# First MLP layer by seven block products, tiles of 512 tokens, decoding in steps: a spectral mixer and MLP on one core

## The chip, the cores and the metric

The kernel runs on one core of a Trainium2 chip. The metric is the time of one execution on the device, in microseconds (us). PE is the engine of matmuls (PEld its weight loads), DVE the vector engine, ACT the scalar (activation) engine, POOL the GpSimd engine, SP the engine that issues the DMAs. SBUF is the memory that the engines work in, PSUM the small one that matmuls write to, in eight banks of 512 float32 columns.

## The reference

There are 8 batches of 3136 tokens with 256 channels. First a spectral stage, then an MLP with a low-rank mixing of tokens (`x` is the output of the first for the second):

```
X = np.fft.rfft(x, axis=1)
Yr = Xr @ w_r - Xi @ w_i + b_r
Yi = Xr @ w_i + Xi @ w_r + b_i
Yr = np.sign(Yr) * np.maximum(np.abs(Yr) - 0.01, 0.0)      # Yi likewise
y  = np.fft.irfft(Yr + 1j * Yi, n=3136, axis=1)

h = xt @ U @ V                       # xt: x with tokens last; U (3136, 32), V (32, 3136)
u = x + h.transpose(0, 2, 1)
ch = np.maximum(u @ w_ch1, 0.0) @ w_ch2      # w_ch1 (256, 1024), w_ch2 (1024, 256)
return u + ch
```

U, V, w_ch1 and w_ch2 come as float64; the kernel turns their words into float32 itself ("decoding").

## The kernel before, in words

Every matmul that needs float32's accuracy is done as three in a cheaper format: an operand is split into a high part (a copy, on ACT) and a low part (the difference, on DVE or POOL), and `mm3` adds high x high, low x high and high x low (lines 93, 94, 95; in the trace these lines stand for all users of the helper, the tiles tell them apart). `split` (lines 82 and 85) makes the two parts.

A batch passes through these stages. **a**: the first step of the transform, 16 units of two of the 32 columns of tokens (`psa`, stored through `gs` to DRAM `gd`). **b**, **mix**, **c**: 12 or 13 pairs `q` of frequencies; `b_unit` loads `t` and the table `fb`, multiplies (`psb`), copies the result out (`xs`), adds real and imaginary parts (`ts`) and splits all three; `mix_unit` does the complex product with the weights by three products (`pst`, `psq`), adds the bias (`tb`), and the shrinking by ACT (`rl`) and DVE (`ys`); `c_unit` does a further step (`psc`) and stores to `zd`. **d**: 32 units (`psd`) finish the inverse transform into `xq` and add up `pa`, the product with U. **MLP**: a tile is 392 tokens (4 x 98); `v_unit` adds the product with V (`psv`) and splits u into `uh`, `ul`; `l1` does one eighth of the first layer, 6 matmuls of 392 columns into `psh`, then ACT takes the relu (`rh`) and DVE its low part (`rlo`, out of PSUM); `l2`, two steps later, does 6 matmuls into the two banks `pso` that gather all eight; at the end `ot` adds u, `os` is transposed, and the result goes out.

The main loop runs over 8 batches x 8 tiles x 8 steps. Beside each step's `l1` and `l2` it emits "side" units: the next batch's b, mix, c (pairs over steps 0 to 36 of 64), a of the batch after, and d (36 to 54). A scheduler then orders all instructions of each engine by a model of their times; on the chip each engine works its list in that order. `behind` and `issue_after` fix an order against it. So batch 0's spectral stage and the decoding have no MLP beside them: this is the run-up, up to the first `psh`.

In the run-up, `decode` takes the words of one piece (`dw`) through 2 operations on ACT and 6 on DVE, or one and one more where the piece is split at once (`dm`, `dlf`, `dq`, `dp`). The pieces of V go to DRAM (`vfl`) and come back spread (`v4`) for `make_v`, which fills `vs`, V for all tokens, in SBUF. U's pieces make `us`; `make_ud` (`psu`) multiplies it into the table of stage d. Four of the eight pieces of the MLP's weights are decoded before the first `psh`, four after it. PSUM has three banks `psf` for the spectral stages, three `psm` (`psh`, `psv`) and the two `pso`.

Of the kernel before, what the change touches and what calls it, by code (L numbers as in the profile page):

```python
# [21 lines left out]
NB = 8  # L22
N1, N2 = 49, 64
NP = 98
# [5 lines left out]
TOK = TI * NP  # L30
# [8 lines left out]
FILL_1, FILL_2, IDLE = 4, 4, 7  # L39
WHOLE_A = {(0, u) for u in range(1, 16)} | {(1, u) for u in range(16)}  # L40

@with_exitstack
def fft_mix_moe_kernel(
# [25 lines left out]
    ps_m = ctx.enter_context(tc.tile_pool(name="ps_m", bufs=3, space=PSUM))  # L69
    ps_o = ctx.enter_context(tc.tile_pool(name="ps_o", bufs=1, space=PSUM))  # L70
    fp = ctx.enter_context(tc.tile_pool(name="fp", bufs=2))
    qp = ctx.enter_context(tc.tile_pool(name="qp", bufs=2))

# [37 lines left out]
    w1s = [const.tile([128, 2, 1024], F32R, name=f"w1{k}") for k in "hl"]  # L111
# [7 lines left out]
    vs = const.tile([128, NI, NP], F32R, name="vs")  # L119

    xv = x.rearrange("b (p i) d -> b p i d", i=NI)

    ov = out.rearrange("b n (a d) -> b a n d", a=4)
    ob = ov[:, :, 0 : 96 * NI].rearrange("b a (p g t) d -> b a t p g d", g=12, t=NT)
    ol = ov[:, :, 96 * NI :].rearrange("b a (q i) d -> b a i q d", i=NI)
    rest = {}
# [4 lines left out]
    first_w = {}  # L131

    def a_load(b, u, ahead=False):
        if ahead:
            xt = qp.tile([NP, 2, D], F32, tag="xq", name=f"xt_{b}_{u}", bufs=10)
        else:
            xt = fp.tile([NP, 2, D], F32, tag="xt", name=f"xt_{b}_{u}")

        late = b == 1 and u >= FILL_1
        with tc.issue_after(s_state[0, "zl"].ins) if late else nullcontext():  # L140
            dma.dma_start(xt, xv[b, :, 2 * u : 2 * u + 2, :])
        a_state[b, u, "x"] = xt

    def a_prep(b, u):
# [6 lines left out]
        xh = fp.tile([NP, 2, D], F32R, tag="xh", name=f"xh_{b}_{u}")  # L151
        xl = fp.tile([NP, 2, D], F32R, tag="xl", name=f"xl_{b}_{u}")
# [3 lines left out]
    def a_mm(b, u):  # L156
# [5 lines left out]
        tg = "xs" if b == 0 and u % 2 else "gs"  # L162
# [10 lines left out]
    def a_units(b):  # L173
        us = []
        for u in range(NI // 2 + 1):
            def unit(u=u):
                if u < NI // 2:
                    a_prep(b, u)
                if u > 0:
                    a_mm(b, u - 1)  # L180
            us.append(unit)
# [17 lines left out]
    def load_fb(b, q):  # L199
# [3 lines left out]
        tg = "fb" if b else ("fb", "th", "tl")[q % 3]  # L203
        fbt = fp.tile([128, 2, 128], F32, tag=tg, name=f"fb_{b}_{q}", bufs=2)
# [19 lines left out]
    def ybuf(b, q, tag):  # L224

        tg, bufs = (tag, 1) if b else (dict(rl="xsh", ys="xsl")[tag], 2)
        return fp.tile([128, 2, D], F32, tag=tg, name=f"{tag}_{b}_{q}", bufs=bufs)

    def b_mm(b, q):
# [3 lines left out]
        pl, tg = (ps_f, "psf") if b else (ps_m, "psm")  # L233
        ps = pl.tile([128, 2, 2, 128], F32, tag=tg, name=f"psb_{b}_{q}")
# [14 lines left out]
    def b_unit0(q):  # L249
        n = pairs(0)[q][1]  # L250
        ps = b_mm(0, q)
        xx = []
        for k in "hl":
            xx.append(qp.tile([128, 2, 2, 3, 64], F32R, tag="xq", name=f"x3{k}_{q}", bufs=10))
        xh, xl = xx
# [13 lines left out]
    def mix_unit0(q):  # L269
        n = pairs(0)[q][1]  # L270
        xx = s_state.pop((0, q, "x"))
        pl, tg = ((ps_f, "psf"), (ps_m, "psm"))[q % 2]
        ps = pl.tile([128, 2, D], F32, tag=tg, name=f"psy_{q}")
# [16 lines left out]
        yh = fp.tile([128, 2, D], F32R, tag="yh", name=f"yh_0_{q}")  # L290
        yl = fp.tile([128, 2, D], F32R, tag="yl", name=f"yl_0_{q}")
# [4 lines left out]
    def b_unit(b, q):  # L296
# [6 lines left out]
        xs = fp.tile([128, 2, 2, 2, 64], F32, tag="xs", name=f"xs_{b}_{q}")  # L303
        for h in range(2):
            acopy(xs[:, h, :, 0:n, :], psv[:, h, :, 0:n, :])
        ts = fp.tile([128, 2, 2, 64], F32, tag="ts", name=f"ts_{b}_{q}", bufs=1)
        pool.tensor_tensor(
            out=ts[:, :, 0:n], in0=xs[:, :, 0, 0:n], in1=xs[:, :, 1, 0:n], op=ALU.add
        )
        xh = fp.tile([128, 2, 2, 2, 64], F32R, tag="xsh", name=f"xsh_{b}_{q}")  # L310
        xl = fp.tile([128, 2, 2, 2, 64], F32R, tag="xsl", name=f"xsl_{b}_{q}")
# [723 lines left out]
```

## Time and profile before

| | |
|---|---|
| median of 3 runs | 1788.68 us (1786.59 to 1791.38) |
| profiled execution | 1784.9 us, span from first to last instruction 1783.1 |
| granted clock of PE | 0.99 |
| PE busy | 1754.8 us, 98% |
| DVE, ACT, POOL busy | 1004.1, 876.7, 546.0 us (56, 49, 31%) |
| DMA | 192 MB, 38% of the 16 engines' time |
| first `psh` | 145 us after the start |

A row of a group reads: line, engine, operation, out<-in, shapes, count | busy us, mean ns of one | idle time before them and what ended it. A row of the timeline reads: start in us, length, engine, line, operation and shape; x2 means that two were merged. In the chain of work that ended last a row has start, length, engine, tile and line.

### The profile page before, as it was taken

What the parts mean: (1) busy time and instruction counts of PE and PEld (TensorE: products, weight loads), DVE (VectorE), ACT (ScalarE), POOL (GpSimd) and SP (SyncE); (2) the same over time, 40 slices, a digit from 0 to 9 for tenths busy, and PEclk for the clock granted to TensorE, in tenths of its full rate; (3) what the DMA queues carried; (4) which work ended last, traced back from release to release, by engine and by line L of the source; (5) the groups of instructions that cost most, each with busy time, mean ns of one, the idle gap of its engine ahead of it and who ended that gap; (6) DMA issues with size and microseconds to landing.
All of it is one profiled execution on the core that took longest, in us unless ns stands there. A gap on an engine that the chain in (4) does not pass through costs nothing.

```text
span 1783.1 us, 30104 instructions
## 1 busy us (share of the span) xinstructions
PE 1754.8 (98%) x10755; PEld 1687.0 (95%) x10755; DVE 1004.1 (56%) x1942; ACT 876.7 (49%) x1879; POOL 546.0 (31%) x583
## 2 busy tenths in 40 slices
PE   8989999999999999999999999999999999999998
PEld 5877999999999999999999999999999999999997
DVE  2667666456643567447653377645664357644443
ACT  3756565455445565344545566444554555443232
POOL 1212453133314464113322455313331334211110
PEclk9979999999999999999999999999999999999999
DMA  7775443423245453322324445332224533240001
GB/s 239 209 224 179 141 135 98 112 77 84 56 120 148 144 156 103 106 69 75 80 74 140 143 139 152 87 101 66 78 63 111 149 102 94 51 118 22 23 23 28
DMA packets 285546, 192.46 MB, mean 108 GB/s; under 512 B 167874, under 2 KB 257222, under 8 KB 285202
## 3 DMA queue, kind: packets, MB, share of 16 engines
q1 hardware_dynamic: 285398, 190.54, 38.4%
q8 instruction: 86, 1.41, 0.3%
q14 instruction: 62, 0.51, 0.1%
HBM read 112.59 MB, written 77.87 MB: 107 GB/s over the span
## 4 chain that ended last, share of the span: by engine, by line
PE 89%; DMA 4%; DVE 3%; SPq 1%; ACT 1%; issue 1%; POOL 0%; DVEq 0%; ACTq 0%; POOLq 0%
PE pso L95 10%; PE psh L93 10%; PE pso L94 10%; PE psh L95 10%; PE pso L93 10%; PE psh L94 10%; PE psd L449 6%; PE psb L237 4%; PE psq L93 2%; PE psq L95 2%; PE psq L94 2%; DMA gd<-gs 1%; PE psv L820 1%; PE psa L94 1%; PE psa L93 1%; PE psa L95 1%
## 5 line engine op out<-in xcount | busy, mean ns | idle before, releaser
L838 DVE SCALAR_TENSOR_TENSOR rlo<-psh,rh 128x392 fp32r<-128x392 f32 x512 | 284.9, 561 | 329.0 <-ACT rh L837 326.4
L837 ACT ACTIVATE rh<-psh 128x392 fp32r<-128x392 f32 x512 | 252.3, 496 | 353.5 <-PE psh L95 271.6
L93 PE MATMUL psh<-uh,w1h 128*128 128x392 f32 x1024 | 352.8, 345 | 0.1
L95 PE MATMUL psh<-uh,w1l 128*128 128x392 f32 x1024 | 350.7, 343 | 0.0
L94 PE MATMUL psh<-ul,w1h 128*128 128x392 f32 x1024 | 350.5, 342 | 0.0
L94 PE MATMUL pso<-rlo,w2h 128*128 128x392 f32 x1024 | 350.2, 342 | 0.0
L95 PE MATMUL pso<-rh,w2l 128*128 128x392 f32 x1024 | 350.2, 343 | 0.0
L93 PE MATMUL pso<-rh,w2h 128*128 128x392 f32 x1024 | 334.0, 346 | 0.0
L85 POOL TENSOR_TENSOR yl<-ys,yh 128x512 fp32r<-128x512 f32 (+1 forms) x101 | 130.9, 1296 | 314.8 <-ACT yh L82 312.5
L85 POOL TENSOR_TENSOR ul<-xq,uh 128x392 fp32r<-128x392 f32 x126 | 133.3, 1067 | 282.2 <-ACT uh L82 282.0
L357 DVE SCALAR_TENSOR_TENSOR ys<-tb,rl 64x256 f32<-64x256 f32 x350 | 181.3, 518 | 61.0 <-ACT rl L353 57.2
L93 PEld LDWEIGHTS pso<-rh,w2h 128*128 128x128 f32 x1024 | 191.2, 188 | 5.8 <-issue 0.7
L93 PEld LDWEIGHTS psh<-uh,w1h 128*128 128x128 f32 x1024 | 192.4, 188 | 4.4 <-DVE rlo L838 0.5
L94 PEld LDWEIGHTS pso<-rlo,w2h 128*128 128x128 f32 x1024 | 192.6, 188 | 3.7
L95 PEld LDWEIGHTS pso<-rh,w2l 128*128 128x128 f32 x1024 | 192.4, 188 | 2.7 <-DVE rlo L838 0.3
L94 PEld LDWEIGHTS psh<-ul,w1h 128*128 128x128 f32 x1024 | 192.6, 188 | 2.4
L95 PEld LDWEIGHTS psh<-uh,w1l 128*128 128x128 f32 x1024 | 192.5, 188 | 2.0 <-issue 0.5
L85 POOL TENSOR_TENSOR xl<-xt,xh 98x512 fp32r<-98x512 f32 x96 | 129.3, 1347 | 169.8 <-ACT xh L82 162.1
L82 ACT ACTIVATE xq<-psd 128x196 f32<-128x196 f32 x256 | 85.1, 335 | 116.2 <-PE psd L449 102.8
L353 ACT ACTIVATE rl<-tb,lam 128x512 f32<-128x512 f32 x88 | 63.5, 721 | 123.3 <-DVE tb L350 123.1
L449 PE MATMUL psd<-dt,zt 98*128 98x130 f32 x896 | 121.2, 274 | 0.0
L449 PEld LDWEIGHTS psd<-dt,zt 98*128 98x128 f32 x896 | 118.9, 190 | 0.0
(161 smaller groups left out, 2920.2 us busy)
## 6 DMA issues: line engine op xcount, KB each, us to landing
xt<-in_x_dram SPq DMA_DIRECT2D x128, 196.0 KB
gd<-gs SPq DMA_DIRECT2D x128, 196.0 KB
zt<-zd SPq DMA_DIRECT2D x128, 196.0 KB
t<-gd SPq DMA_DIRECT2D x192, 128.0 KB
zd<-zs SPq DMA_DIRECT2D x192, 128.0 KB
out_dram<-os SPq DMA_DIRECT2D x256, 96.0 KB
fb<-in_fb_dram SPq DMA_DIRECT2D x96, 128.0 KB
dt<-in_fd_dram SPq DMA_DIRECT2D x56, 150.1 KB
```

The source lines that it names most:

```text
L82: return act.activation(o, i, AF.Copy)
L85: return eng.tensor_tensor(out=o, in0=a, in1=b, op=ALU.subtract)
L93: pe.matmul(o, lhsT=l[0], rhs=r[0], start=first, stop=False)
L94: pe.matmul(o, lhsT=l[0], rhs=r[1], start=False, stop=False)
L95: return pe.matmul(o, lhsT=l[1], rhs=r[0], start=False, stop=last)
L237: pe.matmul(ps[:, h, k, :], lhsT=t[:kk, k, h * 128 : h * 128 + 128], rhs=fbt[:kk, k if k0 else 0, :], start=True, stop=True,)
L353: act.activation(rl[:m], yv[:m], AF.Relu, bias=lam[:m])
L357: dve.scalar_tensor_tensor(out=ys[64 * c : 64 * c + 64, k, :], in0=yv[64 * k : 64 * k + 64, c, :], scalar=LAM, in1=rl[64 * k : 64 * k + 64 ...
L449: pe.matmul(psv[:, h, :], lhsT=zt[:, i % 2, 128 * h : 128 * h + 128], rhs=dt_[:, k, :], start=True, stop=True,)
L820: mm = pe.matmul(ps[:, 0:TOK], lhsT=pt[:, 128 * h : 128 * h + 128], rhs=vt, start=True, stop=True)
L837: act_ = act.activation(rh, o, AF.Relu)
L838: dve_ = dve.scalar_tensor_tensor(out=rl, in0=o, scalar=0.0, in1=f32(rh), op0=ALU.max, op1=ALU.subtract)
```

## The change

**First layer.** With the weight as 2 x 2 blocks (output features in halves of 512, input channels in halves of 128) and a window of 512 tokens as 2 x 2 (channels by token halves of 256), the first layer is done by Winograd's form of Strassen's method: seven block products of 512 features x 128 channels x 256 tokens, where before there were eight. Sums of weight blocks are made once (`combine`, into `w1t`, seven blocks, high and low). Sums of the token blocks are made for each window: t1 = b12 - b11, t2 = b22 - t1, t3 = b22 - b12, t4 = b21 - t2 (`tt`), and these and b11, b21, b22 are split into `oa`, `ob`, `oc`, `od`. A product is still three matmuls for each 128 features. The products are added up partly in PSUM (`psx`, `psy`, `psz`, a bank each) and partly by ACT's copies (`s5`, `s1`, `v12`) and DVE's additions; then the relu and its low part, whose input is now in SBUF for three of four. The features are done in two halves `g`; each half has four chunks c0 to c3, and between them stand the four chunks of the second layer of the half before.

**Windows.** 98 = 96 + 2 rows of tokens: six windows of 16 x 32 tokens for a batch; the remaining 2 x 32 tokens of all batches are gathered in DRAM (`rd`, by `rest_unit`, `psr`) and make a 49th window at the very end. u stays in `xq` (half a batch each, three buffers), and V is loaded for each window (`vw`) from DRAM `vd`, where it lies split.

**Spectral stages.** `b_unit` copies the high parts straight out of PSUM, and DVE makes the low parts and `ts` out of PSUM too (before, ACT copied `xs` and POOL added `ts`). Buffers `xh`, `xl`, `xsh`, `xsl`, `th`, `tl`, `yh`, `yl` are single. The a units of batch 1 are unsplit for 8 of 16, before for all. Side units have other places among 96 slots a batch.

**Decoding.** It is a generator that gives way after one to three instructions; the run-up takes three steps of it behind each pair's mix, eight more behind the last, and one behind every other d unit. All weights are decoded before the first layer starts; a load is issued three jobs ahead.

```
-TOK = TI * NP
+TOK = 512
+HT = TOK // 2
...
-FILL_1, FILL_2, IDLE = 4, 4, 7
-WHOLE_A = {(0, u) for u in range(1, 16)} | {(1, u) for u in range(16)}
+FILL_1, FILL_2, IDLE, STEPS_W = 4, 4, 7, 8
+WHOLE_A = {(0, u) for u in range(1, 16)} | {(1, u) for u in range(FILL_1 + FILL_2)}
...
+        for h in range(2):
+            acopy(xh[:, h, :, 0:n], vs[h])
+            acopy(ts[:, h, 0:n], vs[h][:, 0])
+        for h in range(2):
+            sub(dve, xl[:, h, :, 0:n], vs[h], f32(xh[:, h, :, 0:n]))
+            dve.tensor_tensor(out=ts[:, h, 0:n], in0=ts[:, h, 0:n], in1=vs[h][:, 1], op=ALU.add)
...
+        def decoding():
+            for k, (_, run) in enumerate(jobs):
+                yield from run()
+                if k + 3 < len(jobs):
+                    jobs[k + 3][0]()
+            yield from combine()
...
+        for q in range(13):
+            for k in range(3):
+                after_mix(q, 1.5 + k + (q == 0), steps, 1)
...
+        after_mix(12, 2.6, steps, STEPS_W)
...
+        for n in range(16):
+            on(100.5 + 2 * n, steps, 1)
...
+    def l1(w, g, o, k, name, first, last=False):
+
+        wk = w1t[:, k]
+        r = m_state[w, "o"][name]
+        for j in range(2):
+            c = slice(128 * (2 * g + j), 128 * (2 * g + j) + 128)
+            for n, (lk, rk) in enumerate(((0, 0), (0, 1), (1, 0))):
+                mm = pe.matmul(
+                    o[:, j],
+                    lhsT=wk[:, lk, c],
+                    rhs=r[rk],
...
+        def c0():
+            st["x"] = bank(0, "x")
+            mm = l1(w, g, st["x"], 3, "t1", True)
+            st["s5"] = sv("s5")
+            a = acopy(st["s5"], st["x"])
+            st["y"] = bank(1 + g % 2, "y")
+            l1(w, g, st["y"], 0, "b11", True)
+            st["s1"] = sv("s1")
+            acopy(st["s1"], st["y"])
...
+        def c1():
+            x, y, s1 = st["x"], st["y"], st["s1"]
+            st["z"] = z = bank(2 - g % 2, "z")
+            l1(w, g, z, 1, "b21", True, True)
+            l1(w, g, x, 6, "b22", False, True)
+            l1(w, g, y, 4, "t2", False)
+            dve.tensor_tensor(out=s1, in0=z, in1=s1, op=ALU.add)
+            v = sv("v12")
+            acopy(v, x)
+            dve.tensor_tensor(out=v, in0=v, in1=y, op=ALU.add)
+            rh, rl = r_tiles(0)
+            relu(rh[:, :, 0], rl[:, :, 0], s1)
+            relu(rh[:, :, 1], rl[:, :, 1], v)
...
+        def c2():
+            y, s5 = st["y"], st["s5"]
+            l1(w, g, y, 5, "t3", False)
+            dve.tensor_tensor(out=s5, in0=y, in1=s5, op=ALU.add)
...
+        def c3():
+            y = st["y"]
+            l1(w, g, y, 2, "t4", False, True)
...
-                    start, mid, end = (0, 36, 54) if b else (12, 46, 58)
+                start, mid, end = (1, 54, 80) if b else (18, 69, 86)
```

What stands in the engines' lists now, at three places. First PE near the end, where the MLP runs alone: before, tile 2 of batch 7 (psh is numbered by batch, tile and eighth, pso by batch, tile and half; the last number of a name is the buffer's).

```order
L95 MATMUL psh_7_2_3_19696<-uh_7_2_19580,w1l_89 128x392
L93 MATMUL psh_7_2_4_19713<-uh_7_2_19580,w1h_88 128x392
L94 MATMUL psh_7_2_4_19713<-ul_7_2_19581,w1h_88 128x392
L95 MATMUL psh_7_2_4_19713<-uh_7_2_19580,w1l_89 128x392
...
L93 MATMUL pso_7_2_0_19688<-rh_7_2_0_19639,w2h_90 128x392
L94 MATMUL pso_7_2_0_19688<-rlo_7_2_0_19640,w2h_90 128x392
```

Now, the second half of window 43 and the start of window 44 (psx, psy, psz are numbered by window and half).

```order
L103 MATMUL pso_43_1_20050<-rh_43_0_1_19998,w2h_89 128x512
L104 MATMUL pso_43_1_20050<-rl_43_0_1_19999,w2h_89 128x512
L105 MATMUL pso_43_1_20050<-rh_43_0_1_19998,w2l_90 128x512
L979 MATMUL psy_43_1_20040<-odh_43_19919,w1t_88 128x256
L979 MATMUL psy_43_1_20040<-odl_43_19920,w1t_88 128x256
L979 MATMUL psy_43_1_20040<-odh_43_19919,w1t_88 128x256 x2
...
L979 MATMUL psx_44_0_20150<-och_44_20103,w1t_88 128x256
...
L979 MATMUL psy_44_0_20159<-obh_44_20099,w1t_88 128x256
L103 MATMUL pso_43_0_20049<-rh_43_1_0_20080,w2h_89 128x512
```

First-layer matmuls of 256 columns stand now where those of 392 stood, with second-layer ones of 512 between, and the last turn on psy of one half stands among the first products of the next.

Second DVE where b_unit and mix_unit run beside the MLP: before, tile 1 of batch 4 with pairs 2 and 3 of batch 5.

```order
L838 SCALAR_TENSOR_TENSOR rlo_4_1_0_12274<-psh_4_1_0_12266,rh_4_1_0_12273 128x392
L85 TENSOR_TENSOR xsl_5_2_12035<-xs_5_2_12029,xsh_5_2_12034 128x512
L341 TENSOR_TENSOR tb_5_1_12080<-pst_5_1_12072,bias_92 128x512
L838 SCALAR_TENSOR_TENSOR rlo_4_1_1_12312<-psh_4_1_1_12304,rh_4_1_1_12311 128x392
L350 TENSOR_TENSOR tb_5_1_12080<-tb_5_1_12080,psq_5_1_12073 128x512
```

Now, window 37 (batch 6) with pairs 2 and 3 of batch 7.

```order
L330 TENSOR_TENSOR ts_7_3_17686<-ts_7_3_17686,psb_7_3_17681 128x128
L362 TENSOR_TENSOR tb_7_2_17639<-tb_7_2_17639,psq_7_2_17632 128x512
L1030 TENSOR_TENSOR s1_37_0_17785<-psz_37_0_17821,s1_37_0_17785 128x512
L369 SCALAR_TENSOR_TENSOR ys_7_2_17656<-tb_7_2_17639,rl_7_2_17654 64x256 x4
L1033 TENSOR_TENSOR v12_37_0_17841<-v12_37_0_17841,psy_37_0_17778 128x512
L992 SCALAR_TENSOR_TENSOR rl_37_0_0_17845<-s1_37_0_17785,rh_37_0_0_17844 128x2x256
L992 SCALAR_TENSOR_TENSOR rl_37_0_0_17845<-v12_37_0_17841,rh_37_0_0_17844 128x2x256
L1042 TENSOR_TENSOR s5_37_0_17776<-psy_37_0_17778,s5_37_0_17776 128x512
L353 TENSOR_TENSOR tb_7_3_17743<-pst_7_3_17735,bias_91 128x512
```

Beside rl, which was rlo, stand now s1, v12 and s5, whose results PE waits for (v12 and s5 read psy, to which PE adds next), and the rl read SBUF alone; ts came over from POOL.

Third DVE in the run-up, where ys of a pair ends its mix: before, pairs 9 and 10 with both pieces of U.

```order
L521 TENSOR_TENSOR dp2_u00_918<-dlf_u00_916,dp2_u00_918 98x512
L287 SCALAR_TENSOR_TENSOR ys_0_9_976<-psy_9_948,rl_0_9_974 128x512
L524 TENSOR_TENSOR us_298<-dq_u00_917,dp2_u00_918 98x512
L513 TENSOR_SCALAR dm_u10_982<-dm_u10_982 98x512
...
L521 TENSOR_TENSOR dp2_u10_985<-dlf_u10_983,dp2_u10_985 98x512
L524 TENSOR_TENSOR us_298<-dq_u10_984,dp2_u10_985 98x512
L287 SCALAR_TENSOR_TENSOR ys_0_10_1053<-psy_10_1025,rl_0_10_1051 128x512
```

Now, pairs 7 to 9 with make_v's two subtractions (d2v).

```order
L300 SCALAR_TENSOR_TENSOR ys_0_7_821<-psy_7_793,rl_0_7_819 128x512
L95 TENSOR_TENSOR d2v0_791<-v4_618,d1v0_790 96x512
L95 TENSOR_TENSOR d2v1_844<-v4_618,d1v1_843 96x512
L95 TENSOR_TENSOR w1t_88<-psb_0_9_850,w1t_88 128x4x128
L300 SCALAR_TENSOR_TENSOR ys_0_8_888<-psy_8_860,rl_0_8_886 128x512
L660 SCALAR_TENSOR_TENSOR vr_100<-vr_100,nm_101,vraw_286 128x64
L533 TENSOR_SCALAR dm_210_906<-dm_210_906 128x512
```

U's decoding moved up to pairs 3 to 5, and the sixteen operations of vs became these two and one small one; the run-up's x3 and wi lie in w1t's room, so that the rows into w1t ahead of the first layer are those of b_unit.

More of the change, by code (lines that the diff above doesn't have):

```diff
@@ L573, in fft_mix_moe_kernel @@
         ]
-        wi = [sp.tile([128, 2, D], F32R, name=f"wi{k}") for k in "hl"]
         b4 = wz
@@ L709, in fft_mix_moe_kernel, with steps @@
+        def decoding():
[4 more added lines that the diff above has]
+            yield from combine()
+        todo = decoding()
+        def steps(n):
+            for _ in range(n):
+                if next(todo, 0):
+                    return
         du0 = d_units(0, du)
@@ new lines, in u_rest @@
+    def u_rest(w):
+        m_state.pop((w, "rest"))()
+    def l1(w, g, o, k, name, first, last=False):
[8 more added lines that the diff above has]
+                    rhs=r[rk],
+                    start=first and j == 0 and n == 0,
+                    stop=last and j == 1 and n == 2,
+                    skip_group_check=True,
+                )
+        return mm
@@ L888, in rest_unit @@
[L888 to L897 removed]
+            pe.matmul(
+                ps[:, 64 * h : 64 * h + 64], lhsT=pt[:, 128 * h : 128 * h + 128], rhs=vr, start=True, stop=True
+            )
@@ L956, in _dft_constants @@
+    for c in l2s:
+        c()
 def _dft_constants():
```

664 lines of the change are left out of this document (394 added, 270 removed).

## The prediction

> **What bounds the kernel now.** I read the page first: engines, then the chain that ended last.
>
> ```profile
> span 1783.1 us, 30104 instructions
> ...
> PE 1754.8 (98%) x10755; PEld 1687.0 (95%) x10755; DVE 1004.1 (56%) x1942; ACT 876.7 (49%) x1879; POOL 546.0 (31%) x583
> ...
> PE 89%; DMA 4%; DVE 3%; SPq 1%; ACT 1%; issue 1%; POOL 0%; DVEq 0%; ACTq 0%; POOLq 0%
> ```
>
> PE is the bound: 89% of the chain. DVE is the next engine, and POOL counts because of DVE, as shown below. The busy time of PE says nothing of its speed, since matmuls overlap; the price of a matmul is the distance between starts, which the timeline of PE gives.
>
> ```profile
> 709.60 0.40 PE L93 MATMUL psc<-yh,fch 128*128 128x512 f32 x1
> 709.84 0.40 PE L94 MATMUL psc<-yl,fch 128*128 128x512 f32 x1
> 710.07 0.39 PE L95 MATMUL psc<-yh,fcl 128*128 128x512 f32 x1
> 710.30 0.34 PE L93 MATMUL pso<-rh,w2h 128*128 128x392 f32 x1
> ...
> 802.37 0.34 PE L93 MATMUL psh<-uh,w1h 128*128 128x392 f32 x1
> ...
> 803.44 0.28 PE L93 MATMUL psq<-wm1h,xsh 128*128 128x256 f32 x1
> ...
> 804.50 0.34 PE L93 MATMUL psh<-uh,w1h 128*128 128x392 f32 x1
> ```
>
> Three 512-column matmuls take 0.70 us, so 0.233 each. The six of 392 columns from 802.37 to 803.44 take 0.178 each (0.179 over longer stretches, 801.29 to 803.44 for twelve). The nine of 256 columns to 804.50 take 0.118 each. That is the same price per column at all three widths (0.46 ns), so tiles of 256 columns cost nothing extra, though every one loads other weights.
>
> Next the stages, in stretches of the span (columns: length, then busy us of PE, PEld, DVE, ACT, POOL, then clock, DMA share, GB/s).
>
> ```profile
> 0.00:145.00 145.00, 128.66 (x722) 101.38 (x723) 73.80 (x147) 79.31 (x176) 19.36 (x31) 0.89 0.76 222
> 155.00:175.00 20.00, 19.36 (x88) 15.11 (x87) 16.96 (x29) 12.50 (x24) 5.32 (x4) 1.00 0.49 151
> 1480.00:1520.00 40.00, 40.00 (x265) 39.35 (x264) 29.86 (x51) 22.00 (x49) 17.14 (x18) 1.00 0.35 94
> 1640.00:1760.00 120.00, 120.00 (x673) 120.00 (x672) 51.00 (x95) 34.88 (x69) 15.76 (x20) 1.00 0.09 24
> ```
>
> The run-up lasts to 145 us. After it PE never idles while DVE is up to 75% busy (29.86 of 40); where DVE is 85% busy (16.96 of 20) PE loses 0.64 us of 20, 3.2%. These two rows are my scale for what a busier DVE costs.
>
> **The change, part by part.**
>
> *First layer on PE.* Before: 64 tiles x 8 x 6 = 3072 matmuls of 392 columns, 3072 x 0.179 = 549.9 us. After: 49 windows x 2 halves x 7 products x 6 = 4116 of 256 columns, 4116 x 0.118 = 485.7, or 481.6 by the price per column (117 ns). I take 482.5: **-67.4 us**, all of it on the path. Ends: at 0.118 -64, at 0.116 -72.
>
> *Second layer on PE.* 2352 x 0.233 = 548.0 against 549.9: -1.9 by that row, 0 by price per column. I take -0.5. *psv:* 96 of 512 for 128 of 392, 0; the 16 new psr matmuls have no row; as small ones they are priced by psd below, 0.90 / 8 = 0.11 each, +1.8.
>
> ```profile
> 144.04 1.88 PE L92 MATMUL psa<-xt,fas 98*98 98x512 f32 x4
> ...
> 330.30 0.90 PE psd L449 x8
> ```
>
> Eight groups of psa change from two whole passes, 1.88 / 4 = 0.47 each, to three split ones of 0.233: -1.9 by these, I take -1.5, since records can be missing. Sum of PE: **-67.6**.
>
> *DVE in the MLP.* The order counts, for 512 tokens, 18 operations of 512 columns, 4 of 256 and 2 transposes. The rows of before:
>
> ```profile
> L838 DVE SCALAR_TENSOR_TENSOR rlo<-psh,rh 128x392 fp32r<-128x392 f32 x512 | 284.9, 561 | 329.0 <-ACT rh L837 326.4
> L350 DVE TENSOR_TENSOR tb<-tb,psq 128x512 f32<-128x512 f32 x87 | 59.6, 685 | 28.2 <-PE psq L95 26.1
> L879 DVE STREAM_TRANSPOSE os<-ot 128x384 f32<-128x384 f32 x128 | 86.0, 691 | 0.7
> L480 DVE TENSOR_TENSOR pt<-psp,pt 64x256 fp32r<-64x256 f32 x8 | 3.4, 428 | 6.3 <-ACT pt L82 6.3
> L85 DVE TENSOR_TENSOR x3l<-psb,x3h 128x128 fp32r<-128x128 f32 x2 | 0.6, 292 | 1.1 <-ACT x3h L82 1.1
> ```
>
> After, per window: 18 x 0.685 + 4 x 0.428 + 2 x 0.9 (691 scaled by columns) = 15.9 us. Before, a tile of 392 has 12 x 0.56 + 2 x 0.69 = 8.1, or 10.6 for 512 tokens. That is +5.3 x 49 = +260 us, and in b_unit the two subtractions and two additions out of PSUM (2 x 0.428 + 2 x 0.292 = 1.44) replace one subtraction of 0.945: +0.5 x 88 = +44. DVE goes from 1004 to some 1300 us of a span near 1715: 76% on the mean, and by far more in windows that also run b_unit and mix_unit.
>
> One such is window 37 (batch 6, half 0). There DVE has the 15.9, and 8 xsl of 256, 8 ts of 128, 8 tb of 512 and 20 ys of 64x256, in all 3.4 + 2.3 + 5.5 + 8.6 = 19.8: 35.7 us. PE has for it 84 x 0.117 + 50 x 0.233 + 72 x 0.117 of pst and psq + 10 psc of 0.233 + 12 psb in two passes of 0.11, 35.0. Summed the same way for all windows, DVE reaches 90% of PE's time or more in 17 of 49 (with 0.1 us for POOL, next), 567 us of PE's time together; in the worst (8, 32, 37) it passes it, by 5.6 us in all. But operations that follow at once start earlier than the durations say:
>
> ```profile
> 1488.14 0.68 DVE L85 TENSOR_TENSOR xsl<-xs,xsh 128x512 fp32r<-128x512 f32 x1
> 1488.74 0.68 DVE L341 TENSOR_TENSOR tb<-pst,bias 128x512 f32<-128x512 f32 x1
> ```
>
> They start 0.60 apart at 0.68 each, so a full DVE gains some 10% back. PE is then still the bound, with DVE about 85 to 95% busy in those 17 windows; at the 3.2% of the row 155 to 175 that costs **+18 us**. Ends: 0 (the row at 75%), and 43 in the rival below.
>
> *DVE against POOL.* Where an operation of DVE reads both inputs from SBUF, it is slower beside POOL:
>
> ```profile
> L85 DVE TENSOR_TENSOR xsl<-xs,xsh 128x512 fp32r<-128x512 f32 x87 | 82.2, 945 | 58.1 <-ACT xsh L82 52.9 <-DMA xt<-in_x_dram 2.9 <-DMA t<-gd 2.3
> L85 DVE TENSOR_TENSOR x3l<-psb,x3h 128x512 fp32r<-128x512 f32 x12 | 8.3, 688 | 8.6 <-DMA t<-gd 7.2 <-ACT x3h L82 1.2
> L357 DVE SCALAR_TENSOR_TENSOR ys<-tb,rl 64x256 f32<-64x256 f32 x350 | 181.3, 518 | 61.0 <-ACT rl L353 57.2
> L85 POOL TENSOR_TENSOR yl<-ys,yh 128x512 fp32r<-128x512 f32 x99 | 129.3, 1307 | 309.7 <-ACT yh L82 307.3 <-PE psh L95 2.0
> ```
>
> xsl, which always stands beside POOL's ts, takes 257 ns more than x3l with one input in PSUM; ys, at any time, takes 518, 90 more than the 428 of pt. The change raises the number of such operations from 437 to 836 (294 rl that read s1, v12 or s5, 192 of tt, 350 ys). I take 0.1 each, as for ys, which is in the 18 us. POOL itself stays near 560 us (ul 133 becomes 3.5 splits a window, 225; ts and rest, 85, go).
>
> The Trainium skill, "SBUF — State Buffer", section "SBUF: two separate sides", calls this an exclusive lock: a DVE operation with two SBUF inputs and a GpSimd operation that reads SBUF hold the shared port for a whole instruction, and the other blocks. With POOL busy 31% and half of 1.3 us left on the mean, that would be an estimated 0.2 us each, the excess over PE 25 us instead of 6, and the time 20 us longer than my sum. The mean of ys bears out half of it.
>
> *The run-up.* V's decoding and spreading stands on the chain there:
>
> ```profile
> 53.68 3.87 DMA vfl<-full
> ...
> 58.23 4.30 DMA vfl<-full
> ...
> 77.56 4.39 DMA v<-vfl
> 82.03 1.89 ACT vs L82 x4
> ...
> 86.81 1.71 DVE dq_u L515
> ```
>
> These 16 us block in-order queues; PE's rows ahead of the first psh, at the prices above, sum to 109 of the 145 us. The change replaces vs (16 copies and 16 operations on DVE in turn) by two splits whose load is issued three jobs ahead, and puts one to four decoding rows between ys and the next subtraction: perhaps -10. Against that all eight W pieces and the combining (9 operations of 0.69 on DVE) now stand ahead of the first layer, where before four pieces came after it: +6. Sum **-4**, ends -14 and +8.
>
> *The rest at no price:* 96 vw loads of 128 KB are issued nine slots (some 18 us) before psv reads them; SP issues 1355 DMAs for 1335. xh, xl, xsh and yh with one buffer are rewritten only after PE's matmuls on them, which PE has already passed in the order. Their cover is PE's order; if a split on POOL is late, psa waits. psb keeps one of three psf banks until DVE's four operations: late DVE delays pst next. The end has wider last operations and eight output DMAs for eight small ones after four: +1.5.
>
> **Sum:** 1783.1 - 67.6 - 4 + 18 + 1.5 = 1731.0 us of span; the profiled execution has 1.8 more around it (1784.9) and the median lies 3.8 above that (1788.68): 1736.6, so **1737 us**.
>
> **Rivals.** *DVE becomes the bound with b_unit and mix_unit in the window, but keeps some gain.* For it: window 37 stands at 35.7 against 35.0 before any wait, and each half has three turns PE-DVE-PE through one bank (psy, v12, psy, s5, psy) with some 1.4 us of second layer between. At xsl's 0.26 each the windows' excess sums to 43 us: 1731 + 43 + 5.6 = 1780. Against: the 10% that close operations gain. Range 1756 to 1783. *The lock decides and the kernel is slower:* place, rl and ys beside POOL's splits of u; at 0.35 each the excess is 83 us, the time near 1810. It decides from some 0.3 each (about 60 us, which with the 18 makes up for the 72 that PE and the run-up give); that is more than xsl shows at its worst place, which speaks against. *256-column matmuls cost more in the first layer:* gone is the gain at 549.9 / 4116 = 133.6 ns; the psq rows at 118 nearly exclude it. *The run-up loses less than nothing and DVE none:* 1709 to 1718, if the spreading gives 14 and the 18 fails to come.
>
> **How the numbers follow.** The forecast (1718 to 1755) has 0.57, DVE as bound with gain left 0.18, the good end 0.05: faster by over 0.3% 0.80. Within 0.3% (5.4 us, about what this measurement can tell from no change) 0.06, slower 0.14, by the lock or another wait. The range, 1712 to 1790, leaves out the slow rival and the best end.
>
> **What would show it.** Right: psx, psy, psz 4116 times with 256 columns at about 117 ns; DVE near 1300 us; PE's share of the chain still over 80%; first psx near 141 us. Wrong: groups of psy or pst with tens of us of idle before them, ended by DVE v12, s5 or ts; rl with SBUF inputs means over 0.9 us; the chain with DVE over 15%; the first psx later than 153.

## The result, and the profile after

The changed kernel takes **2028.95 us** (median of 4 runs, 2026.96 to 2032.07) where the kernel before took 1787.63 beside it: 1.135 times as long, 95% interval 1.132 to 1.138. The forecast was 1737, the range ended at 1790. The work of PE fell as forecast, but PE stood still far longer, and ran slower after it. The page of the profile after, its head and one line each of its parts 4 and 5:

```profile
span 2027.5 us, 31494 instructions
PE 1819.8 (90%) x11071; PEld 1586.9 (78%) x11071; DVE 1305.3 (64%) x2476; ACT 1025.6 (51%) x2206; POOL 563.5 (28%) x508
PE 17%; DVE 1%; ACT 1%; DMA 0%; issue 0%; POOL 0%; DVEq 0%; SPq 0%; ACTq 0%; POOLq 0%
L979 PE MATMUL psy<-odh,w1t 128*128 128x256 f32 x784 | 175.9, 286 | 1.9 <-DVE v L1033 1.8
```

PE is 208 us short of the span (28 before). The shares of the chain add up to a fifth only, so this chain can't be used here. The last row is one of the new first layer: 1.9 us of idle time in all ahead of its 784 matmuls. So the waits stand elsewhere. PE's waits, by what was waited for (us in total, times, longest):

```profile
PE psc L103 <- ACT yh L92: 61.8, 21, 6.3
PE psd L469 <- DMA zt<-zd: 41.0, 7, 7.7
PE pst L103 <- ACT th L92: 14.6, 12, 3.7
PE psa L103 <- ACT xh L92: 9.2, 8, 1.2
...
PE psx L979 <- ACT s L92: 6.6, 10, 0.8
```

All of the large ones belong to the spectral side units (c, d, mix, a), not to the first layer. Stretches of the span (PE, PEld, DVE, ACT, POOL busy; granted clock of PE; DMA share; GB/s), the first with b, mix and c beside the first layer, the second, at the end, with the first layer alone:

```profile
300.00:400.00 100.00, 84.72 (x540) 75.66 (x540) 66.24 (x131) 49.73 (x113) 29.93 (x28) 0.93 0.40 102
1900.00:2027.00 127.00, 119.25 (x730) 105.36 (x728) 77.56 (x120) 53.70 (x96) 22.85 (x20) 0.99 0.16 29
```

Alone, the seven products run at full pace: windows 44 to 47 last 22.0, 21.2, 21.1 and 21.2 us from first `psx` to first `psx`, without a wait of PE. Beside b, mix and c DVE has a third of its time free, and PE still waits.

One such wait, in the timeline (start, length, engine, line, operation; in brackets the idle time before and what ended it):

```profile
807.67 0.28 PE L105 MATMUL pst<-wm0h,tl 128*128 128x256 f32 x1
807.79 0.61 PE L251 MATMUL psb<-fb,t 128*128 128x128 f32 x4
...
808.71 0.69 DVE L362 TENSOR_TENSOR tb<-tb,psq 128x512 f32<-128x512 f32 x1
...
809.44 0.72 ACT L365 ACTIVATE rl<-tb,lam 128x512 f32<-128x512 f32 x1
809.46 0.51 PE L933 MATMUL psv<-vw,pt 128*128 128x512 f32 x1 [0.22 <-DVE tb L362]
...
811.91 2.64 DVE L369 SCALAR_TENSOR_TENSOR ys<-tb,rl 64x256 f32<-64x256 f32 x4
...
814.58 0.63 ACT L92 ACTIVATE yh<-ys 128x512 fp32r<-128x512 f32 x1 [2.47 <-DVE ys L369]
...
815.26 0.79 PE L103 MATMUL psc<-yh,fch 128*128 128x512 f32 x1 [5.30 <-ACT yh L92]
815.86 0.41 PE L103 MATMUL pst<-wm0h,th 128*128 128x256 f32 x1
```

The last matmul of mix ends at 807.95. From there `tb`, `rl`, `ys` and `yh` take until 815.2. PE's list has four `psb` and two `psv` in between, about 1 us of work, and then the `psc` that needs `yh`. No row of the first layer is there: window 14's was done, and window 15's (its first `psx` at 819.5) begins only after these `psv` have been added to u, and the sums made and split. The other price is in the last row: 0.41 for a matmul that takes 0.28 elsewhere. The granted clock of PE is 0.50 from 812.5 to 819.3.

From the first `psx` or `psh` to the end, each matmul at its usual spacing (0.117 for 256 columns, 0.179 for 392, 0.233 for 512), the two traces add up thus ("the rest" holds also the 8 to 9 us behind the last matmul):

| us | before | after | difference |
|---|---|---|---|
| run-up, to the first psh or psx | 145.4 | 153.9 | +8.5 |
| PE's rows at their usual spacing | 1618.2 | 1550.8 | -67.4 |
| PE between two matmuls, idle | 3.3 | 178.3 | +175.0 |
| the rest: matmuls slower than usual | 16.2 | 144.5 | +128.3 |
| span | 1783.1 | 2027.5 | +244.4 |

### The profile page after: what moved, and what is told of

It reads as the page before. It is cut to its first block, busy times and chain, and to the rows that moved or that the text cites. A ratio compares the mean times of both kernels' runs of the same rounds, so it can differ in the third digit from the quotient of the medians.

```text
span 2027.5 us, 31494 instructions
## 1 busy us (share of the span) xinstructions
PE 1819.8 (90%) x11071; PEld 1586.9 (78%) x11071; DVE 1305.3 (64%) x2476; ACT 1025.6 (51%) x2206; POOL 563.5 (28%) x508
## 5 line engine op out<-in xcount | busy, mean ns | idle before, releaser
L104 PE MATMUL pso<-rl,w2h 128*128 128x512 f32 x784 | 311.1, 397 | 0.2
L105 PE MATMUL pso<-rh,w2l 128*128 128x512 f32 x784 | 310.3, 396 | 0.0
L103 PE MATMUL pso<-rh,w2h 128*128 128x512 f32 x784 | 283.5, 398 | 1.9 <-ACT rh L991 1.9
L992 DVE SCALAR_TENSOR_TENSOR rl<-s,rh 128x512 fp32r<-128x512 f32 x196 | 146.0, 755 | 50.3 <-ACT rh L991 47.7
L979 PE MATMUL psy<-odh,w1t 128*128 128x256 f32 x784 | 175.9, 286 | 1.9 <-DVE v L1033 1.8
L991 ACT ACTIVATE rh<-s 128x512 fp32r<-128x512 f32 x196 | 120.7, 629 | 102.0 <-DVE s L1030 75.2
L104 PEld LDWEIGHTS pso<-rl,w2h 128*128 128x128 f32 x784 | 147.3, 188 | 29.8 <-DVE rl L992 2.1
L979 PEld LDWEIGHTS psy<-odh,w1t 128*128 128x128 f32 x784 | 134.4, 188 | 8.4 <-DVE v L1033 3.6
L251 PE MATMUL psb<-fb,t 128*128 128x128 f32 (+1 forms) x800 | 112.9, 284 | 8.9 <-DMA t<-gd 8.1
L979 PE MATMUL psy<-odl,w1t 128*128 128x256 f32 x392 | 110.9, 283 | 0.0
```

Of the source, the lines that this page charges most:

```text
L103: pe.matmul(o, lhsT=l[0], rhs=r[0], start=first, stop=False)
L104: pe.matmul(o, lhsT=l[0], rhs=r[1], start=False, stop=False)
L105: return pe.matmul(o, lhsT=l[1], rhs=r[0], start=False, stop=last)
L251: pe.matmul(ps[:, h, k, :], lhsT=t[:kk, k, h * 128 : h * 128 + 128], rhs=fbt[:kk, k if k0 else 0, :], start=True, stop=True,)
L979: mm = pe.matmul(o[:, j], lhsT=wk[:, lk, c], rhs=r[rk], start=first and j == 0 and n == 0, stop=last and j == 1 and n == 2,  skip_group_ch ...
L991: a = act.activation(rh, v, AF.Relu)
```

## Experiments

Three theories stand in the expectations. **A**: the next window's `psv` now takes its turn in the `psf` banks behind the side units, so the first layer runs dry. **B**: the seven products themselves, by DVE's load and their turns PE-DVE-PE. **C**: the change turned the order of the side units round, to c, mix, b, since the single buffers allow no other: c of a pair then follows its mix two units later instead of four, and so does mix its b. In the built order the PE work between a pair's last `psb` and its first `pst` has a median of 10.9 us before and 5.5 after; between its last `psq` or `pst` and its first `psc`, 10.7 and 6.5. (In the expectation of e3 rows of 392 columns were priced at 0.233; at their own 0.179 its figures are 10.9 to 6.6 and 10.7 to 7.2. Counted in the traces of before and after, the medians are 10.9 and 5.1, 11.0 and 6.0.) Ratios are to the kernel before, run beside each.

### The changed kernel with one part undone

**e1**, `psv` out of `psf`:

```diff
-                ps = ps_f.tile([128, TOK], F32, tag="psf", name=f"psv_{w}_{h}")
+                ps = ps_m.tile([128, TOK], F32, tag=f"psm{h}", name=f"psv_{w}_{h}")
```

> Only edit: the two products of V for the next window (psv) are written to the banks psm0 and psm1 instead of taking turns in the three psf banks with the spectral stages. Theory A (in the changed kernel the next window's preparation waits in psf behind the side units, so the main loop runs out of work and PE waits on the side chain): about 1850 us, the waits psc<-yh fall from 61.8 us to under 25. Theory B (the seven-product layer itself, by DVE's load and its turns PE-DVE-PE): within 20 us of 2029. Theory C (the side units' reversed order with single buffers leaves the chain b, mix, c too little cover): 1980 to 2030, and psc<-yh stays over 45 us.

1974.22 us, ratio 1.107 (1.102 to 1.111): 55 us less, so A is a part of it, a quarter and not the whole. `psc<-yh` still waits 41.0 us. Time and wait lie between what A and C had named, so no theory was met in full.

**e2**, eight block products in the first layer again:

```diff
-        tt = mp.tile([128, 2, HT], F32, tag="tt", name=f"tt_{w}")
...
+                mm = mm3(
+                    o,
+                    [w1t[:, 2 * i + h, k, c] for k in range(2)],
+                    [t.rearrange("p k n -> p (k n)") for t in m_state[w, "o"][h]],
+                    h == 0,
+                    h == 1,
+                )
```

> The first layer is done by eight block products again (six matmuls of 512 columns for each 128 features, relu and its low part straight out of PSUM, no t sums; three psm banks in turn); windows of 512, side units, buffers and the psf banks stay as in the changed kernel. PE's own work is then 548 us in the first layer instead of 482, some 1731 us in all by the same prices. Theory B: about 1800 us, since DVE's work and turns of the seven products are gone. Theories A and C: 1980 to 2080, PE waits for psc<-yh and psd<-zt as in the changed kernel.

2130.54 us, ratio 1.194 (1.190 to 1.197). That is 102 us *more* than with seven products, and B falls: the new first layer is the part that gains, and everything else in the change loses 345 (2130.54 against 1785.41 beside it). DVE is busy 979.6 us, less than in the kernel before, and PE waits longer than ever:

```profile
PE 1880.2 (88%) x9307; PEld 1532.2 (72%) x9307; DVE 979.6 (46%) x1978; ACT 828.3 (39%) x1811; POOL 449.9 (21%) x411
PE psc L103 <- ACT yh L92: 106.7, 35, 6.0
PE psd L469 <- DMA zt<-zd: 44.3, 7, 7.5
```

**e4**, `psv` and the sums t1, t2 six slots earlier:

```diff
-                        if 8 * g + 2 * k + c == 10:
+                        if 8 * g + 2 * k + c == (4 if (w + 1) % NW else 10):
                             u_prep(w + 1)
+                        if 8 * g + 2 * k + c == 10:
+                            m_state.pop((w + 1, "more"))()
```

> In the changed kernel the first part of u_prep (psv, the additions to u and the sums t1 and t2 in tt) moves from slot 10 of a window to slot 4, except ahead of a batch's first window; the splits stay at slot 10, since their buffers are free only then. Theory A: psv then stands in psf ahead of six slots of side units, so about 1930 us. Theory B: within 20 us of 2029. Theory C: 2000 to 2030.

2034.35 us, ratio 1.139 (1.136 to 1.143): nothing gained. (This is what B had said too, but e2 speaks against B.) `psc<-yh` fell to 49.2 us, but `psa<-xh` rose to 21.6 and `psx<-oah` to 15.0: the splits of `oa` can't go earlier than their buffers come free. A, in the form that an early place is enough, falls.

### The kernel before with one part of the change

**e3**, the order of the side units for batches 1 to 7, buffers still double:

```diff
-            if q < nq:
-                us.append(ub)
+            units = [ub] if q < nq else []
...
+            us += units[::-1] if b else units
```

> The kernel before with one edit of the change: for batches 1 to 7 the side units are emitted in the order c, mix, b instead of b, mix, c (buffers stay double). In the built order this cuts PE's work between psb and its pst from 13 to 8.4 us and between psq and its psc from 12.5 to 9.2 us. Theory C, where the order alone does it: 1830 us or more, with waits psc<-yh of 20 us or more. Theories A and B: within 10 us of 1788.

1872.44 us, ratio 1.048 (1.046 to 1.051). Turning three units round costs 87 us in the old kernel. C has its place, though the waits are not all where it put them:

```profile
PE psd L449 <- DMA dt<-dud: 18.0, 13, 3.0
PE psd L449 <- DMA zt<-zd: 16.1, 3, 5.4
PE psa L93 <- ACT xh L82: 5.3, 3, 2.3
```

Only 3.5 us stand at `psc`; the chain comes late as a whole, and d, which needs all of it, seems to run with too little first layer left beside it. That is read from the waits; no run tested it.

**e6**, `psv` in `psf`:

```diff
-            ps = ps_m.tile([128, 512], F32, tag="psm", name=f"psv_{b}_{t}_{h}")
+            ps = ps_f.tile([128, 512], F32, tag="psf", name=f"psv_{b}_{t}_{h}")
```

> The kernel before with psv in the three psf banks instead of psm. Theory A alone: 1830 us or more, as half of what was regained by undoing it in the changed kernel. Theory C: within 12 us of 1786, since in the old order nothing in psf waits long and the first layer has eleven more steps of work.

1804.05 us, ratio 1.009 (1.007 to 1.010): 16 us, between the two forecasts; it met neither.

**e7**, `b_unit` out of PSUM (`xs` and POOL's `ts` gone):

```diff
-            acopy(xs[:, h, :, 0:n, :], psv[:, h, :, 0:n, :])
+            acopy(xh[:, h, :, 0:n], vs_[h])
+            acopy(ts[:, h, 0:n], vs_[h][:, 0])
+        for h in range(2):
+            sub(dve, xl[:, h, :, 0:n], vs_[h], f32(xh[:, h, :, 0:n]))
+            dve.tensor_tensor(out=ts[:, h, 0:n], in0=ts[:, h, 0:n], in1=vs_[h][:, 1], op=ALU.add)
```

> The kernel before with the changed kernel's way out of PSUM in b_unit: ACT copies the high parts and the first term of ts, DVE makes xsl and ts from PSUM in four operations; POOL's ts and ACT's xs are gone. DVE some 1050 us instead of 1004. Theory C: within 10 us of 1786 (the chain is a copy shorter). Rival: psb keeps its psf bank until DVE's fourth operation, so pst and psa come late: 1800 or more.

1785.86 us, ratio 0.998 (0.997 to 1.000): no cost, within 0.3%.

**e8**, e3, e6 and e7 at once:

> The kernel before with three parts of the change at once: the side units' order c, mix, b (alone it gave 1872), psv in psf and b_unit out of PSUM; first layer, tiles of 392, buffers and slots as before. If the parts only add, 1870 to 1900. If they compound, because a side chain with little cover now also holds up psv and with it the first layer: 1930 or more.

1971.69 us, ratio 1.103 (1.101 to 1.104). Alone they cost 87, 16 and -2 us, 101 together; at once 184. They compound: the built order now has 5.7 us of PE work (6.6 in e3) between `psb` and `pst`, and 5.7 between mix and `psc`. The waits show d starting straight behind the last c:

```profile
PE psd L445 <- DMA zt<-zd: 35.0, 6, 6.5
PE psc L93 <- ACT yh L82: 17.0, 22, 2.2
PE psh L93 <- ACT uh L82: 7.2, 9, 1.5
```

The third row, with `psv<-tb` (5.4), is the first layer waiting, in the old eight-product form.

**e16** and **e17**, the changed kernel's a units (split and matmuls of a unit next to each other, one buffer), alone and with e8:

```diff
+            for u in range(NI // 2):
+                us += [lambda u=u: a_prep(b, u), lambda u=u: a_mm(b, u)]
```

> The kernel before with the changed kernel's a units for batches 2 to 7: each unit's split of x and its matmuls are emitted next to each other, and xh, xl keep one of their two buffers (before, unit u is split ahead of the matmuls of u-1). If cover is the rule here too, psa waits for ACT's xh and POOL's xl, some 1.9 us for each of 96 units less what stands between: 1810 to 1850. If the first layer fills it: within 10 us of 1787.

> The three parts of e8 (order c, mix, b; psv in psf; b_unit out of PSUM; together 1972) and the a units of e16. If the a units add to the same chain of waits: 2020 or more, toward the 2130 of e2, which has the same work of PE. If not: 1965 to 1990.

1784.64 us, ratio 0.999 (0.998 to 1.000), and 1979.12, ratio 1.108 (1.106 to 1.111). Alone the a units cost nothing; with the rest some 7 to 10 us, by the times or by the ratios.

### The changed kernel with cover given back

**e5** and **e9**: a second buffer for `yh` and `yl`, the order mix, b, c, and `psv` in `psm`; e5 also spreads b, mix and c to slot 60 and starts d three slots behind.

```diff
-            us += units[::-1] if b else units
+                us += mixes + bs + cs
...
-            fp.tile([128, 2, D], F32R, tag=f"y{k}", name=f"y{k}_{b}_{q}", bufs=1) for k in "hl"
+            (first_w["mp"] if q % 2 else fp).tile([128, 2, D], F32R, tag=f"y{k}", name=f"y{k}_{b}_{q}", bufs=1)
```

> The changed kernel with the side chain loosened: yh and yl get a second buffer, the side units are emitted mix, b, c (in the built order 13 us of PE's work instead of 6.5 then stand between psq and its psc, 6 us as before between psb and its pst), d starts three slots behind the last c and the b, mix and c units are spread to slot 60 instead of 54, and psv has the banks psm0 and psm1. (sv has three buffers, tt shares vw's.) Theory C (cover of the side chain): under 1890 us, psc<-yh under 15 us, psd<-zt under 10. If what is left comes from the turns of the first layer and DVE's load, 1930 to 1975.

> As e5 (two buffers of yh and yl, order mix, b, c, psv in psm), but b, mix and c end at slot 54 and d at 80 as in the changed kernel. In e5 the windows 5, 17, 29 and 41, in which d ran with the first layer already waiting for the next batch, lasted 91, 61, 64 and 44 us instead of some 34 or 22. If the later slots did that: 1800 to 1850. If it is the chain's own pace, whatever the slots: 1865 to 1890.

1876.31 us, ratio 1.050 (1.048 to 1.052), and 1878.45, ratio 1.051 (1.048 to 1.053): 150 us of the 241 come back by this alone, with the seven products untouched, and the later slots of e5 make no difference. Both lie where C, or the chain's own pace, had put them. In e9 `psc<-yh` is down to

```profile
PE psc L103 <- ACT yh L92: 8.1, 6, 4.0
```

What is left stands at the ends of batches: the first layer is through, and the next batch's d is not. Windows 5, 17, 29 and 41 of e9 last 97, 66, 63 and 44 us.

**e10**, **e11**, **e12**: e9 with earlier side units (b, mix, c to slot 50 or 48, d to 72 or 70), and e10 with one low part of the relu in four taken from DVE:

```diff
-                start, mid, end = (1, 54, 80) if b else (18, 69, 86)
+                start, mid, end = (1, 50, 72) if b else (18, 64, 80)
...
-            relu(rh[:, :, 0], rl[:, :, 0], s1)
+            act.activation(s1, s1, AF.Relu)
+            split(rh[:, :, 0], rl[:, :, 0], s1, pool)
```

> As e9 with the side units still earlier: b, mix, c to slot 50 (batch 1: 64), d three slots later to 72 (80). If windows 5, 17, 29 and 41 lose their waits: 1760 to 1800. If DVE, with 4 instead of 3.7 pairs in a window, becomes the bound there: 1800 to 1850.

> As e10 with b, mix, c to slot 48 (62) and d to 70 (80): within 10 us of e10 where the place of the slots is no longer what binds, 15 us or more below it where it still is.

> As e10, with one of four low parts of the relu (of s1) taken from DVE to POOL: ACT takes the relu of s1 in place and copies the high part, POOL subtracts. DVE loses 98 operations of 0.69 us (68 us), ACT gains 98 of 0.6, POOL 98 of 1.3. Theory B's remainder (DVE's load binds where b, mix and c run): 15 to 40 us below e10. Else within 10 us of it or slower, by POOL's longer operation ahead of the second layer.

1872.01 us (ratio 1.047, 1.043 to 1.051), 1886.47 (1.057, 1.053 to 1.062) and 1905.65 (1.067, 1.064 to 1.070). e10 and e11 met none of their forecasts. Earlier slots move the waits only: in e10 windows 5 and 29 last 86 and 85 us. Taking load off DVE (e12) made it 34 us slower than e10, where B would have had it 15 to 40 faster. With e2 this is the second result against B, but a weaker one: the edit also gives 98 operations each to ACT and POOL, which the side chain passes too.

**e13**, **e14**, **e15**: the old order b, mix, c and two buffers for `xsh`, `xsl`, `th`, `tl`, `yh`, `yl` (one less of `gs`, `zs`, `fb` and `sv`), `psv` in `psm`; e14 with eight products, e15 with `psv` in `psf`:

```diff
-            us += units[::-1] if b else units
+            us += units
...
-            fp.tile([128, 2, 2, 2, 64], F32R, tag=f"xs{k}", name=f"xs{k}_{b}_{q}", bufs=1) for k in "hl"
+            fp.tile([128, 2, 2, 2, 64], F32R, tag=tg, name=f"xs{k}_{b}_{q}", bufs=1)
+            for k, tg in zip("hl", ("gs2", "zs2") if q % 2 else ("xsh", "xsl"))
```

> The changed kernel with the chain's cover of before: xsh, xsl, th, tl, yh, yl have two buffers for batches 1 to 7 (the room comes from one buffer less of gs, zs, fb and sv), the side units stand in the order b, mix, c, psv has psm0 and psm1; slots as in the changed kernel. In the built order 10 us of PE's work stand between psb and pst and 10.6 between psq and psc (5.5 and 6.5 in the changed kernel). Theory C, the chain's cover is the whole of the loss: under 1790 us, near 1750. Theory B for the rest: 1850 to 1880, as e9.

> As e13 with eight block products in the first layer (as in e2). Theory C: 60 to 100 us above e13, by PE's 66 us more. Theory B: below e13 or level with it.

> As e13 with psv in the psf banks again. If psf only passes the chain's waits on, it costs little once the chain has cover: within 25 us of e13 (16 us in the old kernel, e6). If it costs by itself: 40 to 60 us, as in e1.

1861.75 us (ratio 1.041, 1.038 to 1.044), 1919.70 (1.074, 1.071 to 1.077) and 1863.78 (1.043, 1.040 to 1.045). Three things follow. The seven products gain 58 us here and 102 between e2 and the changed kernel; their 66 to 67 us less of PE work stand between. e13 lies in the range given to B for the rest, but e14, 58 us above it and not below, speaks against B. With the cover given back, `psv` in `psf` costs nothing (2 us, within the runs' spread), where without it cost 55: here `psf` for the most part passes the chain's lateness on to the first layer. Not all of it, perhaps: in the old kernel, with its full cover, it cost 16 (e6). And the theory that cover is all of it missed: I expected 1790 or less. e13's page still shows

```profile
PE 1759.2 (94%) x11071; PEld 1547.5 (83%) x11071; DVE 1312.5 (70%) x2476; ACT 1027.8 (55%) x2206; POOL 575.5 (31%) x508
PE psb L251 <- DMA t<-gd: 22.0, 4, 6.7
PE psa L103 <- ACT xh L92: 11.8, 13, 1.3
PE psd L474 <- DMA dt<-dud: 7.1, 5, 2.3
```

Counted as in the table above, it has 81 us of idle PE and 82 of slow matmuls behind the run-up. Over half of that, 94 us, was lost in four windows: 12, 24 and 36 (the first of batches 2, 4 and 6) lost 24, 24 and 23, window 5 lost 22. In each of the first three the side units begin b of the next batch, and one wait stands out: for `t`, which reads what stage a of that batch has just stored. In window 12:

```profile
625.05 0.31 SPq L186 DMA_DIRECT2D gd<-gs  x1
...
627.33 0.61 SPq L226 DMA_DIRECT2D t<-gd  x1
...
630.97 2.05 PE L251 MATMUL psb<-fb,t 128*128 128x128 f32 x8 [6.63 <-DMA t<-gd]
```

PE's granted clock is 0.50 for 14 to 21 us around each. The kernel before takes this way through DRAM as slowly, 7.2 us from a's last store for batch 3 (586.8) to the first `psb` (594.0), but PE is busy all the while: a chain again whose cover is gone. **Still open** is what makes up the 73 us by which e13 stands above the kernel before (131 with eight products, e14). Beside that passage from a to b it can be the buffers that e13 itself took from `gs`, `zs`, `fb` and `sv`, or parts that no run took alone: the preparation of windows of 512 tokens, the places of the units among 96 slots, and the larger pieces that each engine then works in order. No version was found that beats the kernel before; e7 and e16 are level with it.

## Why the prediction was wrong

*PE's rows: right.* Forecast -67.6 (with the small rows); the table has -67.4. It uses the forecast's prices, so the close agreement is one of counts. The price shows in the spacing of `psx`, `psy` and `psz`: a median of 118 ns against the 117 assumed, some 4 us over 4116 matmuls, which disposes of the rival of dearer 256-column matmuls. The rows of `psx` (durations min/median/max, first and last start):

```profile
L979 PE MATMUL psx<-oah,w1t x392: 274/281/583, 153.9 to 2001.7; 128*128 128x256 f32 x196
```

*The run-up: wrong by sign.* -4 was forecast, ends -14 and +8; the first `psx` starts at 153.9 against 145.4, +8.5, past the 153 that was to show it wrong. This was not followed further.

*DVE's load: right.* 1305.3 us against some 1300. The price of POOL beside it, 0.1 us for each operation with two inputs in SBUF, was right for `rl` and too low for `tt`:

```profile
L992 DVE SCALAR_TENSOR_TENSOR rl<-s,rh 128x512 fp32r<-128x512 f32 x196 | 146.0, 755 | 50.3 <-ACT rh L991 47.7
L992 DVE SCALAR_TENSOR_TENSOR rl<-v,rh 128x512 fp32r<-128x512 f32 x98 | 80.9, 825 | 22.1 <-ACT rh L991 19.5
L992 DVE SCALAR_TENSOR_TENSOR rl<-psy,rh 128x512 fp32r<-128x512 f32 x98 | 67.3, 687 | 38.3 <-ACT rh L991 37.8
L95 DVE TENSOR_TENSOR tt<-xq 128x256 f32<-128x256 f32 x96 | 79.0, 822 | 52.7 <-POOL oal L95 47.2 <-POOL odl L95 4.9
```

`rl` from SBUF takes 68 and 138 ns more than from PSUM. `tt`, which stands where POOL splits u, has a median of 427 in the row shown and a mean of 822; the slower quarter takes 1.4 us and more. The Trainium skill, "SBUF — State Buffer", section "SBUF: two separate sides", has the whole instruction wait in such a case. `tt` bears that out: of all 192, 44 took over 1.2 us, and 43 of these started while one of POOL's subtractions (`obl` or `xl`) ran and ended within 0.35 us after it. What PE lost by it no run shows apart; that DVE's load decides, as the slower rival near 1810 had it, does not fit e2, which has a quarter less of DVE's work and is slower. (The sum of the first rival, 1780, has both the 18 us and the 43 that were to take their place; without the 18 it is 1762.)

*PE's waits: the term that failed.* +18 us was put for it, ends 0 and 43. It is 175 idle and 128 of slow matmuls, 303, or 285 more than the term; with the 12 by which the run-up missed, this is the miss of the forecast. The term was sized by a rule from one row, that a window loses where DVE nears PE: in the stretch 155 to 175 of the kernel before, with DVE at 85%, PE lost 0.64 us of 20. But the waits of that stretch were there to be read, and what PE waited for was not DVE but a load of x:

```profile
PE psa L92 <- DMA xt<-in_x_dram: 0.5, 2, 0.3
```

The trace after denies the rule as well. There DVE was busy for 90% or more of the time of PE's own rows in 16 of the windows 1 to 47; these lost 112 us over those rows, the other 31 lost 196. Windows 8, 18, 30 and 32, at 90 to 92%, lost 1 to 2 each, windows 11 and 35, at 70%, 10 and 13. What parts them is the side work in them. In the seven windows in which c passes over to d (4, 9, 15, 21, 27, 33, 39) 9 to 13 us each were lost, 80 together; in the ten with a units beside b, mix and c 7 to 29 each, 132 together; with b, mix and c but neither a nor d 1 to 11; with d alone or nothing beside the first layer (16, 28, 40, 42 to 47) 1.3 at most. I took load for latency: DVE's 64% says nothing of how long a result takes that passes PE, DVE, ACT, DVE, ACT and PE again. How long can be read in both traces: from a pair's last matmul of mix to the end of its `yh` the median is 4.9 us before and 5.4 after, over 6.3 and 7.0 in one pair of ten.

*The step at no price: the mistake behind it.* "Their cover is PE's order", said of the single buffers, was right as a sentence; but the order itself had been changed in the same lines (`us += units[::-1]`), and the cover it gives had gone from 10.9 and 10.7 us of PE work to 5.5 and 6.5. With 11 us of cover, `psc` started 5.3 us after the end of its `yh` (median); with 6, 0.9 us after it, so that a small delay of the chain became a wait of PE. The order of before and after was there to be compared, and of the places looked at none was the chain from `psb` to `psc`. The second half, that late DVE delays what waits for a `psf` bank, was named without a price; with `psv` behind it in the same banks it is one way by which the lateness reached the first layer (55 us, e1).

*The rivals.* None was this one. Lateness was expected in the first layer's turns, with `psy` or `pst` waiting for DVE's `v12`, `s5` or `ts`; the first layer's `psy` waits under 5 us in all, and windows 44 to 47 show the turns at full pace. "Another wait" was in the slower case's 0.14, without a mechanism.

*Why the loss is 303 and not 175.* Of the 128 us, 86 were lost by matmuls while the granted clock was 0.50, as the last section shows. Some 22 more are a matter of counting: the last matmul ahead of each of some 150 waits counts with its whole length. The remaining 20 are not explained.

## What to carry to other kernels

When a change makes buffers single, ask what order of work that forces, and count for each chain through several engines how much of the bound engine's work now stands between its steps; compare that with the chain's length in the trace, not with any engine's busy share. A change that only gains where the engine is fed can lose more by what comes with it: here seven products gave 58 to 102 us, and the rest of the change cost 345 (e2), of which 214 came back with the old order, second buffers and other banks for `psv` (e14). A bank or a buffer that main and side work share can make the side work's waits the main work's.

## What the runs showed of the hardware

PE pays twice for a wait. Stretches of 2 us around a wait for `yh` in the changed kernel (same columns as above):

```profile
696.00:698.00 2.00, 1.44 (x10) 0.91 (x8) 0.95 (x2) 0.88 (x5) 0.00 (x0) 1.00 0.62 106
698.00:700.00 2.00, 0.00 (x0) 0.00 (x0) 1.84 (x6) 2.00 (x5) 0.14 (x1) 0.95 0.86 226
700.00:702.00 2.00, 0.00 (x0) 0.00 (x0) 1.97 (x3) 0.03 (x1) 2.00 (x2) 0.50 0.93 227
702.00:704.00 2.00, 0.96 (x3) 0.86 (x4) 0.33 (x1) 0.63 (x1) 0.98 (x2) 0.50 0.37 105
704.00:706.00 2.00, 2.00 (x12) 2.00 (x11) 0.00 (x0) 0.00 (x0) 0.34 (x1) 0.50 0.00 0
706.00:708.00 2.00, 1.77 (x10) 1.33 (x9) 0.67 (x1) 0.20 (x1) 0.00 (x0) 0.84 0.00 0
708.00:710.00 2.00, 1.92 (x12) 1.66 (x13) 1.41 (x5) 1.56 (x4) 0.00 (x0) 1.00 0.14 31
```

The gap begins at 697.4 and work comes back at 703.0. The granted clock falls to 0.50 at 699.8, 2.4 us into the gap, and is full again at 706.6, 3.6 us after work came back. All 14 gaps of 5 us or more behind the run-up are followed by 3 to 9 us of matmuls at half pace. The Trainium skill, "TensorE: Matmul & The Clock Gate", section "Part 1: The HAM clock gate", describes such a gate, with an idle or busy window of some 3.4 us both ways. The trace agrees as to the length: 31 of its 32 stretches at 0.50 behind the run-up last 3.4 us or two to four times that. It differs in that less than a whole window of idle time was enough, 2.4 us in the gap above. PE need not even be idle at a stretch:

```profile
655.00:657.00 2.00, 0.79 (x4) 0.19 (x2) 1.72 (x3) 1.12 (x2) 0.28 (x1) 1.00 0.03 8
657.00:659.00 2.00, 0.86 (x3) 0.25 (x2) 0.00 (x0) 0.22 (x1) 0.98 (x1) 0.96 0.88 205
659.00:661.00 2.00, 1.05 (x3) 0.79 (x3) 0.00 (x0) 0.89 (x2) 1.03 (x1) 0.50 0.97 230
```

The clock fell at 658.9. In the 3.4 us before, PE had gaps of 1.21 and 0.88 us and the start of a third, and was busy for about a third of the time. It then stayed at 0.50 for 10.2 us, though PE was busy for half of the time and more.
